# Linear attention with a bilinear feed-forward: the opening four units rescheduled (scaling on VectorE alone, idle matmuls in the kv bank, natural-k transposes together)

## The chip, the cores and the metric

One core of a Trainium2 chip runs the whole program. Times are device microseconds of an execution. A run is called slow when it is over 1.5% above the fastest of the same kernel. The kernel before needs 238.9 us (median of 3 runs, 238.88 to 238.95). Each profile is of one execution, and its clock starts at the first instruction of the span (237.3 us before).

## The reference, cut to what matters

```python
# B, H, S, D = 4, 8, 768, 64; decay lam per head
for b in range(nb):                                   # blocks of a sequence
    intra = einsum('bhic,bhjc->bhij', qb, kb) * Dmask     # lower triangle, lam**(i-j)
    intra = einsum('bhij,bhjd->bhid', intra, vb)
    inter = einsum('bhid,bhde->bhie', qb * lam_pow, kv_state)
    out[:, :, sl] = intra + inter
    kv_state = lam_block * kv_state + einsum('bhsd,bhse->bhde', kb * rev_pow, vb)
x = out.transpose(0, 2, 1, 3).reshape(B * S, H * D)       # 3072 x 512
y = ((x @ w_a) * (x @ w_b)) @ w_out                       # d_ff = 1536
```

The kernel works on 24 units of 128 rows (6 for each of 4 sequences). It scales q by lam to a power and k by lam to minus that power, so that the mask is a plain triangle. The feed-forward takes the units in groups of 4, 1, 2, 4, 4, 4, 4, 1; attention of later units is woven into the feed-forward of earlier ones. Only the first four units have nothing to hide behind. They are the **opening**, and the change is in it.

## The kernel before

PSUM, the memory that TensorE writes its results to, is handed out as seven banks in rotation (`ps_bank`) and an eighth for the kv states (`kv_bank`). A held bank is left out of the rotation. SBUF is the on-chip memory that holds the operands. An idle matmul (`warm`) is one whose result nobody reads.

```python
    def ps_bank(name, shape, dt, hold=False, ffn=False):
        i = bank["next"]
        while i in bank["held"] or (ffn and i == bank["ffn"]):
            i = (i + 1) % 7
        ...
    idle_ps = ps_bank("idle", [128, 512], F32, hold=True)   # target of idle matmuls: warm(n)
```

The opening itself: four packed inputs (q and k, half of the heads each) are scaled, by VectorE for three of four blocks and by GpSimd for the fourth, transposed on TensorE and copied to SBUF by ScalarE. Then come the scores, the natural-layout k, the states, and the outputs.

```python
        for eng, rs in ((nc.vector, slice(0, 3)), (nc.gpsimd, slice(3, 4))):      # in scale4
            ...eng.tensor_mul(...)
    ...
    for i in range(2):
        scale4("k", i); transpose4("k", i); warm(4)          # cut: one call per line; q likewise
    for u in range(n0):
        make_vb(u, "pool")
    scores4(0)                    # 16 matmuls into 4 banks, then 4 masks on VectorE
    natural_k(0, "act")           # 8 transposes into 1 bank, copied by ScalarE
    warm(4)
    scores4(1)
    natural_k(1, "act")
    sts = [ps_bank("kv0", ...), ps_bank("kv1", ...), kv_bank()]
    for hh in range(2):
        for u, ps in enumerate(sts):
            for w in range(u + 1):
                kv_mms(ps, w, range(2 * hh, 2 * hh + 2), w == 0)
            if hh:
                kv_copy(u, ps, ("act", "dve", "act")[u])
    for u in range(n0):
        inter(u); intra(u); warm(2)                          # cut: one call per line
        evac_o(u, *xTs[u], eng="dve" if u == 2 else "act")
    cast_w("a", 0, "both")        # half on VectorE, half on GpSimd
```

Outside the opening, until unit 6, the k of a unit is scaled on VectorE; q always, and k from unit 7 on, on GpSimd:

```python
    def prep_k(u):
        early = u < n0 + 3
        make_ks(u, "dve" if early else "pool")
        make_qs(u, "pool")
```

## Time and profile before

| what | value | read from |
|---|---|---|
| time, span | 238.9 us, 237.3 us | runs, page |
| TensorE busy | 227.0 us, 96% | page, part 1 |
| VectorE starts on the last k input | 10.35 us | timeline |
| first feed-forward matmul | 21.41 us | timeline |
| last ScalarE copy of the program | 233.99 to 234.26 us | timeline |

A line of the timeline reads: start, duration (of merged instructions, from first to last), engine and line of the code, operation, output<-input and form, and in brackets how long the engine had idled and what ended that. PE is TensorE's matmuls, PEld its weight loads, DVE is VectorE, ACT is ScalarE, POOL is GpSimd, and SPq the queue that issues the DMAs. The chain of waits goes back from the last instruction to what released it, step by step. The lines of before stand in the prediction below. Its state copies, which the change also moves, are these in the timeline:

```profile
17.57 0.74 ACT L371 CAST st<-kv 64x256 bf16<-64x256 f32 x2 [0.44 <-POOL wa_sb L159]
17.81 0.69 DVE L373 TENSOR_TENSOR st<-kv,bdiag 128x512 bf16<-128x512 f32 x1
```

kv1's copy on VectorE (second line) starts when the eighth mask ends.

### The profile page before, as it was taken

The page shows a single profiled execution, that of the slowest core. Times are in us where ns is not written, and L with a number is a line of the kernel's source. Part 1 is how long each engine was busy: PE and PEld are TensorE (multiplying, and loading weights), DVE is VectorE, ACT ScalarE, POOL GpSimd, SP SyncE. Part 2 cuts the span into 40 slices and gives each one's busy share as a digit, 9 for nine tenths or more (in the row PEclk, how much of TensorE's full clock was granted, in tenths as well). Part 3 has the DMA queues.
Part 4 walks back from the last instruction along what each step waited for, and adds up shares of the span by engine and source line. Part 5 has one row for each costly group of instructions (what it writes and reads, how often), then busy time and mean ns, then how long its engine had stood idle before and what let it go on. Part 6 is the DMA issues. An engine that isn't in the chain of part 4 may idle for free.

```text
span 237.3 us, 4532 instructions
## 1 busy us (share of the span) xinstructions
PE 227.0 (96%) x1758; PEld 126.8 (53%) x1781; DVE 113.5 (48%) x202; ACT 92.5 (39%) x171; POOL 53.6 (23%) x66
## 2 busy tenths in 40 slices
PE   7689999999999999999999999999999999999994
PEld 2365444447787754454554454544454544444493
DVE  0684656734647755775145575035565115332050
ACT  3556575037454542332133332143242242332161
POOL 6940001334334544203304503003300000000000
PEclk9999999999999999999999999999999999999999
DMA  4999999999969999995838939513220210000311
GB/s 156 298 291 349 350 369 281 285 217 297 212 157 209 220 185 241 251 196 105 187 125 197 199 64 241 133 57 89 44 47 0 88 69 24 0 0 3 128 48 47
DMA packets 94277, 38.31 MB, mean 161 GB/s; under 512 B 81200, under 2 KB 89776, under 8 KB 94256
## 3 DMA queue, kind: packets, MB, share of 16 engines
q1 hardware_dynamic: 94112, 38.02, 68.5%
q8 instruction: 14, 0.23, 0.4%
q14 instruction: 7, 0.06, 0.1%
q10 hardware_dynamic: 144, 0.00, 0.0%
HBM read 28.32 MB, written 6.29 MB: 146 GB/s over the span
## 4 chain that ended last, share of the span: by engine, by line
PE 88%; DMA 5%; ACT 2%; DVE 2%; issue 1%; SPq 1%; POOL 1%; DVEq 0%
PE a_ps L405 26%; PE b_ps L405 26%; PE op L426 26%; DMA k<-in_k_dram 3%; PE o_ps L337 3%; PE kq L308 2%; PE kvd L351 2%; PE o_ps L329 2%; DVE m L320 1%; DMA out_dram<-o_sb 1%; PE tps L294 1%; ACT o_sb L421 1%; SPq L206 1%; POOL scratch L495 1%; ACT xT L344 0%
## 5 line engine op out<-in xcount | busy, mean ns | idle before, releaser
L417 DVE TENSOR_TENSOR ab<-a_sb,b_ps 128x512 bf16<-128x512 bf16 (+2 forms) x96 | 52.4, 552 | 83.9 <-PE b_ps L405 62.3
L405 PE MATMUL a_ps<-xT,wa_sb 128*128 128x512 bf16 (+2 forms) x378 | 76.6, 325 | 1.4 <-ACT xT L344 0.6
L405 PE MATMUL b_ps<-xT,wb_sb 128*128 128x512 bf16 (+2 forms) x379 | 76.7, 325 | 0.2
L412 ACT CAST a_sb<-a_ps 128x512 bf16<-128x512 f32 (+2 forms) x96 | 45.5, 480 | 66.6 <-PE a_ps L405 64.7
L426 PE MATMUL op<-wo_sb,ab 128*128 128x512 bf16 (+2 forms) x300 | 64.3, 362 | 0.9 <-issue 0.5
L405 PEld LDWEIGHTS <-wb_sb 128*128 128x128 bf16 x384 | 34.5, 98 | 28.8 <-issue 0.2
L405 PEld LDWEIGHTS <-wa_sb 128*128 128x128 bf16 x384 | 33.6, 98 | 28.0 <-issue 1.1
L426 PEld LDWEIGHTS <-ab 128*128 128x128 bf16 x312 | 28.6, 98 | 30.2
L320 DVE TENSOR_TENSOR m<-kq,lotri 128x512 bf16<-128x512 f32 x48 | 29.8, 681 | 22.1 <-PE kq L308 20.4
L256 POOL TENSOR_TENSOR qk<-kf,lp_k 128x512 bf16<-128x512 f32 x17 | 17.9, 1051 | 80.2 <-issue 31.4
L421 ACT COPY o_sb<-op 128x512 f32<-128x512 f32 (+2 forms) x26 | 14.2, 553 | 37.2 <-PE op L426 36.7
L261 POOL TENSOR_TENSOR qk<-qf,lp_q 128x512 bf16<-128x512 f32 x20 | 22.0, 1099 | 23.8 <-DMA qf<-in_q_dram 23.8
L344 ACT CAST xT<-o_ps 128x512 bf16<-128x512 f32 x23 | 12.5, 589 | 17.0 <-PE o_ps L337 17.0
L373 DVE TENSOR_TENSOR st<-kvd,bdiag 128x512 bf16<-128x512 f32 x17 | 11.6, 682 | 3.8 <-PE kvd L351 3.8
L296 ACT COPY qkT<-tps 128x1024 bf16<-128x1024 bf16 x7 | 7.1, 1012 | 11.2 <-PE tps L294 11.2
L194 PE MATMUL idle<-idle_sb 128*128 128x128 bf16 (+1 forms) x41 | 8.2, 334 | 1.3 <-DVE idle_sb L189 1.3
L270 DVE CAST vb<-vf 128x512 bf16<-128x512 f32 x17 | 8.5, 499 | 0.0
L337 PE MATMUL o_ps<-m,vb 128*64 128x128 bf16 x192 | 8.2, 223 | 0.0
L329 PEld LDWEIGHTS <-st 128*128 128x128 bf16 x80 | 5.5, 98 | 2.6
L270 POOL CAST vb<-vf 128x512 bf16<-128x512 f32 x7 | 4.7, 673 | 8.7 <-DMA vf<-in_v_dram 8.7
L337 PEld LDWEIGHTS <-vb 128*64 128x64 bf16 x192 | 5.8, 109 | 1.6
L308 PE MATMUL kq<-qkT 64*128 64x128 bf16 x160 | 6.6, 218 | 0.0
(56 smaller groups left out, 88.9 us busy)
## 6 DMA issues: line engine op xcount, KB each, us to landing
vf<-in_v_dram SPq DMA_DIRECT2D x24, 256.0 KB, 5.0
out_dram<-o_sb SPq DMA_DIRECT2D x23, 256.0 KB, 2.2
qf<-in_q_dram SPq DMA_DIRECT2D x20, 256.0 KB, 4.4
kf<-in_k_dram SPq DMA_DIRECT2D x20, 256.0 KB, 4.6
wst<-in_moe_w_a_dram SPq DMA_DIRECT2D x6, 512.0 KB, 8.7
wst<-in_moe_w_b_dram SPq DMA_DIRECT2D x6, 512.0 KB, 8.7
wst<-in_moe_w_out_dram SPq DMA_DIRECT2D x6, 512.0 KB, 8.4
q<-in_q_dram SPq DMA_DIRECT2D x2, 512.0 KB, 5.5
```

The lines of the kernel that those rows point to most:

```text
L256: eng_of(eng).tensor_mul(qk[:, 1], raw.pop((u, "k")), lp_k[:, u % NB].to_broadcast([128, H, D]))
L261: eng_of(eng).tensor_mul(U[u]["qk"][:, 0], raw.pop((u, "q")), lp_q[:, u % NB].to_broadcast([128, H, D]))
L270: eng_of(eng).tensor_copy(vb, vf)
L320: nc.vector.tensor_mul(m, kq[i], lotri_bc)
L337: nc.tensor.matmul(d["o"][p, hp, :], lhsT=d["vb"][:, 2 * hp + i, :], rhs=d["m"](i, hp), start=(u % NB == 0 and hp == 0), stop=True, skip_g ...
L344: nc.scalar.copy(xT[:, :, col:col + BLK], o_ps)
L373: nc.vector.tensor_mul(st[:].rearrange("p hp i d -> p hp (i d)"), ps[:].rearrange("p hp i d -> p hp (i d)"), bdiag_bc)
L405: nc.tensor.matmul(ps[:, :gt], lhsT=w_sb[:, s, f * 128:(f + 1) * 128], rhs=xT[:, s, :gt], start=(s == 0), stop=(s == KS - 1))
L412: nc.scalar.copy(a_sb[:, :gt], ps[:, :gt])
L417: nc.vector.tensor_mul(ab[:, f, :gt], a_sb[:, :gt], ps[:, :gt])
L421: nc.scalar.copy(o_sb[:, lo:hi], op[:, lo:hi])
L426: nc.tensor.matmul(op[:, lo:hi], lhsT=ab[:, f, t * 128:(t + 1) * 128], rhs=wo_sb[:, f, lo:hi], start=(f == 0), stop=(f == FC - 1))
```

## The change

Intent: get the feed-forward started earlier. VectorE scales alone, in two parts per input, so that transposes of the first part can begin while the second is scaled. The idle matmuls write into the kv bank, which is unused until then, so that the rotation has seven banks. Both natural-k transposes go ahead of the second scores. kv1 is copied by ScalarE and kv2 by VectorE, twelve idle matmuls fall away, and GpSimd casts the whole first weight chunk.

```diff
-        elif eng == "both":
-            nc.vector.tensor_copy(dst[:, :, :128], t[:, :, :128])
+        elif eng == "pool":
+            nc.gpsimd.tensor_copy(dst[:, :, :128], t[:, :, :128])
...
-    idle_ps = ps_bank("idle", [128, 512], F32, hold=True)
+    idle_ps = kvps_pool.tile([128, 512], F32, name="idle", tag="kvd")
...
+    def load4(w, i):                       # in place of scale4 and transpose4
+        ...
+        for j in range(2):
+            hs = slice(4 * i + 2 * j, 4 * i + 2 * j + 2)
+            nc.vector.tensor_mul(...)      # 128 x 512
+            for r in range(PACK):
+                nc.tensor.transpose(tps[:, j, r, :], ..., ident)
...
+    for w in "qk":
+        for i in range(2):
+            load4(w, i)
+            warm(4)
...
     natural_k(0, "act")
-    warm(4)
+    natural_k(1, "act")
     scores4(1)
-    natural_k(1, "act")
...
-                kv_copy(u, ps, ("act", "dve", "act")[u])
+                kv_copy(u, ps, ("act", "act", "dve")[u])
...
-        warm(2)
...
-    cast_w("a", 0, "both")
+    cast_w("a", 0, "pool")
```

## The prediction

> **What bounds the kernel now.** I began with the page of the whole run. Its busy lines say that TensorE carries the kernel:
>
> ```profile
> PE 227.0 (96%) x1758; PEld 126.8 (53%) x1781; DVE 113.5 (48%) x202; ACT 92.5 (39%) x171; POOL 53.6 (23%) x66
> ...
> PEclk9999999999999999999999999999999999999999
> ```
>
> TensorE is busy for 96% of 237.3 us at full granted clock. From the first feed-forward matmul on it hardly waits: the view of TensorE's waits after 21 us lists 0.6 + 0.3 + 0.2 us. So the change, which touches only the first four units, can only move the moment at which that long stretch starts. Second view: the timeline of the opening, at the place where it starts.
>
> ```profile
> 20.60 0.42 DVE L158 CAST wa_sb<-wst 128x512 bf16<-128x512 f32 x1
> 20.78 0.58 ACT L344 CAST xT<-o_ps 128x512 bf16<-128x512 f32 x1 [0.59 <-PE o_ps L337]
> 21.41 1.89 PE L405 MATMUL a_ps<-xT,wa_sb 128*128 128x512 bf16 x7 [0.46 <-ACT xT L344]
> ```
>
> The feed-forward starts at 21.41 us, released by the last xT copy (ended 21.36); the VectorE half of the first weight cast ended at 21.02, just before. Third view: the chain of work that ended last, cut to the opening, names what leads to 21.41.
>
> ```profile
> 2.39 7.93 DMA k<-in_k_dram
> ...
> 10.40 1.39 POOL scratch L495
> ...
> 11.84 0.45 PE tk L505 x5
> 12.29 0.22 PE idle L194 x4
> 12.51 0.38 PE kq L533 x8
> ...
> 12.95 2.49 DVE m L320 x4
> 15.44 0.04 issue
> 15.48 0.62 PE tn L513 x8
> ...
> 16.12 1.02 ACT scratch L518
> ...
> 17.19 0.51 PE kv L351 x6
> ```
>
> The reader is to see three things: GpSimd's quarter of the scaling (1.39) is in the chain although VectorE does three quarters in 0.96; the second natural-k transpose (tn) waits for the fourth mask, because its PSUM bank is the one that mask reads; and its copy on ScalarE (1.02) then stands ahead of the second half of the kv matmuls. After that four units follow at 0.79 us each (17.96, 18.75, 19.54, 20.32), two idle matmuls in each.
>
> **What the Trainium skill says.** "SBUF — State Buffer", section Who interferes with whom: a VectorE instruction with two SBUF inputs contends with a GpSimd instruction that reads SBUF, and the loser waits for the whole instruction. The trace agrees: GpSimd scaled 256 elements in 1.38 us here, but 512 elements in 1.04 us elsewhere (L256); 1.38 is VectorE's 0.96 plus 0.42. "VectorE: DVE Perf Modes", section The TRN2 errata, gives an fp32 tensor_tensor (N+151)/0.96 ns: 957 for 768 and 691 for 512; the trace has 959 (L495) and 683 (L256 on VectorE). "TensorE: Matmul & The Clock Gate", section Step-by-step: matmuls stay in program order and only weight loads are pulled ahead; the trace agrees in that the kv matmuls, whose first inputs were there, came only after tn. The same page, HAM oscillation: the clock halves after a pause of about 3.4 us. No pause that long is in this trace after the start (clock 1.00 in all windows), so it shows neither side.
>
> **Part by part, as a new schedule of the opening.** I take durations, and the gaps after a release (0.05 to 0.06 us), from the rows above.
>
> Scaling. VectorE now does two parts of 512 elements. Eight masks of 512 took 4.87 us in a row, 0.61 apiece, 0.69 for a last one; so two parts take 0.61 + 0.69 = 1.30, and the first is ready after 0.69. The loads are not moved: VectorE waited for each of the four inputs (ready at 5.92, 7.29, 8.85, 10.35), and 10.15, the end of k0's second part, is before 10.35. k1's second part ends at 11.65; its four transposes start at 11.71. Before, the last five started at 11.83. The first transposes of scores now follow 0.55 later (was 0.61, one transpose of 0.056 less): 12.26 instead of 12.44. **Gain 0.18.** Copy of tk1: 12.15 to 13.16. Masks start at 12.77 and end at 12.77 + 7 x 0.61 + 0.69 = 17.7.
>
> Banks. With the idle matmuls in the kv bank, seven banks rotate instead of six. By the code: q in 0,1; k in 2,3; first scores 4,5,6,0; natural k in 1 and 2; second scores 3,4,5,6; kv0 in 0, kv1 in 1; outputs in 2,3,4,5. So natural k waits for no mask. Its two sets of transposes run at 12.81 and 13.26 (the second needs the tk1 copy, 13.16 + 0.06: in time). ScalarE copies them at 13.47 to 14.48 and 14.45 to 15.46; before, the second ended at 17.13. The second scores start at 13.71, wait for mask 3 (12.77 + 2 x 0.61 + 0.69 = 14.68) and end about 15.0.
>
> kv. kv0 sits in bank 0, which mask 4 frees at 12.77 + 3 x 0.61 + 0.69 = 15.29; so the wait for **mask 4 stays, now ahead of kv**. The 24 matmuls run from 15.36 without the pause in the middle: halves at 15.36 and 16.05 (each 12 x 0.056, about 0.70), end 16.75. Before, the second half started at 17.19. **Gain here 1.14** (the 0.18 is inside).
>
> States and outputs. Output 0 needs masks 5 and 6 (16.5): 16.75. kv0 on ScalarE starts 0.38 after the second half begins, as before (17.57 - 17.19): 16.43 to 17.17; kv1 is now on ScalarE too: to 17.91; kvd on VectorE behind the masks: 17.64 to 18.33. Without the two idle matmuls a unit needs about 0.66 instead of 0.79 (0.32 inter, from 18.43 to 18.75; 0.34 intra, from 18.75 to 19.09). Unit 1 starts at 17.23, unit 2 waits for kv1's copy, 17.97, and unit 3 follows at 18.63 (its state is there at 18.39); its intra part runs at 18.95, against 20.32 before. **Gain 1.37**; the ScalarE state copies cost two short waits in it, 0.13 us before unit 1 and 0.08 before unit 2.
>
> Start of the feed-forward. The last copy starts 0.46 after its intra part (before 20.78 - 20.32): 19.41, ends 20.00; first matmul 20.05. The first weight cast is two GpSimd pieces of 0.61 from its landing at 16.88: 18.10, so no longer near the gate. VectorE's second cast (wb) runs after output 2 (18.75 to 19.44) to 20.12; it is needed 1.73 later. 21.41 - 20.05 = **1.36 us**.
>
> After the start. The weights land at about 512 KB per 1.5 us (350 GB/s in the page's row) from 16.88, an estimate: the second a-chunk at 19.9, wanted at 23.7; each later one has more room, as TensorE uses one per 1.73. Then unit 4: its q landed at 40.74, v at 45.74, and its transposes ran at 48.83, so 1.36 earlier still leaves both in time. The last two output-weight casts, which ran at 45.0, may wait some tenths for their load, but their matmuls come at about 50.6. Bank numbers shift by three modulo seven, in the same order. So nothing gives the 1.36 back: 238.9 - 1.36 = 237.54, rounded to **237.5 us**.
>
> **Rivals.** (1) *The wait is replaced.* The masks stay on VectorE for 4.9 us and mask 4 still gates kv; ScalarE then holds four copies in a row for kv0 and kv1. If the kv copies or the mask-bound second scores take longer than in my schedule, the gain is 0.5 to 0.9: 238.0 to 238.4. For it: VectorE has no idle time between 12.95 and 18.5. Against: its end moves 0.2 only, but it stood at 17.8, 3.6 us ahead of the start of the feed-forward.
> (2) *Transfers hide it.* From 45 to 60 us the loads of units 5 to 7 are the slow side (GpSimd waits 1.8, 0.5, 1.5, 1.9 us for them). If the earlier feed-forward runs into them, the gain vanishes: 238.9. Against: TensorE needs unit 5 at 56.2 and unit 6 at 59.6, with k5 and k6 scaled on VectorE behind other VectorE work, without a load wait.
> (3) *The clock.* Fewer idle matmuls might let the granted clock fall. Twelve idle matmuls fall away (0.056 each, 0.7 us of activity in all); my schedule has no pause over 0.8 us between 12 and 20 us. If it happened, one halved window of 3.4 us would cost 1.7 us: 239.3. Chance 3%.
> (4) *More.* If the idle matmuls and gaps count for more than their issue time, the start could be at 19.6: 237.0.
>
> **Range and chances.** My schedule is the most likely; rival 1 at a third, giving 0.4 to 0.8 less, and rival 4 at a tenth. Range 236.9 to 238.4. For 2% the time must move by 4.8 us; the whole stretch from the last load to the feed-forward is 11 us, of which 4.9 are masks that stay. Faster by 2%: 0.01. Slower by 2%: 0.01. Within: 0.98.
>
> **What would show it.** Scaling rows on VectorE of 512 elements near 690 ns, none on GpSimd; the tk1 copy at 12.15; second natural-k copy ended by 15.5; kv matmuls in one row of 24 from about 15.4, released by a mask; kv1 on ScalarE ended near 17.9; first a_ps matmul at 20.05, released by ScalarE's xT copy. At 60 us and later everything should be earlier by the same 1.4. If the feed-forward starts earlier but the span does not follow, rival 2 is right; if the start moves by under 1.0, the schedule failed at the step whose time differs first; a PEclk digit under 9 would be rival 3.

## The result, and the profile after

The changed kernel took 237.97 us (median of 4 runs, 237.75 to 238.28) against 238.93 us in the same rounds; ratio 0.9959 with a 95% interval of 0.9942 to 0.9976. A ratio is the mean time of one kernel's fast runs over that of the other's of the same rounds, so not quite the ratio of the medians. It is clear of 1, below 2%, and within the range. A second measurement of the same kernel (below) gave 0.9944.

The chain of waits of the changed kernel in the opening, to be laid beside that of before:

```profile
2.39 7.90 DMA k<-in_k_dram
...
10.32 1.31 DVE scratch L495 x2
...
11.67 0.40 PE tk L500 x4
12.07 0.22 PE idle L194 x4
12.29 0.55 PE kq L530 x16
12.84 0.57 PE tn L510 x8
13.41 0.02 issue
13.43 1.94 ACT scratch L515 x2
15.37 0.48 PE kv L351 x6
```

GpSimd is gone from it, and the transposes tn no longer stand behind four masks. Both their copies (1.94 us) now run beside the second scores and the wait for the masks. The timeline at the end of the opening:

```profile
15.32 1.35 PEld L351 LDWEIGHTS <-scratch 128*128 128x128 bf16 x24 [0.45 <-issue]
...
16.39 1.51 ACT L371 CAST st<-kv 64x256 bf16<-64x256 f32 x4 [1.03 <-PE kv L351]
...
19.35 0.68 DVE L161 CAST wb_sb<-wst 128x1024 bf16<-128x1024 f32 x1
19.42 0.59 ACT L344 CAST xT<-o_ps 128x512 bf16<-128x512 f32 x1 [0.41 <-PE o_ps L337]
...
20.06 1.89 PE L405 MATMUL a_ps<-xT,wa_sb 128*128 128x512 bf16 x8 [0.68 <-DVE wb_sb L161]
```

All 24 kv weight loads are one row from 15.32. The first of them started before ScalarE's copies ended at 15.37, so it cannot have waited for them, though the chain says so. What it waited for is in the single records of the trace: mask 4 ended at 15.21, and TensorE's queue then had an instruction from 15.25 to 15.30 that waits on the semaphore of the masks. The feed-forward starts at 20.06 us, 1.35 us earlier. TensorE's busy share is again 96%:

```profile
PE 227.6 (96%) x1769; PEld 126.3 (53%) x1769; DVE 116.5 (49%) x205; ACT 92.4 (39%) x171; POOL 48.8 (21%) x63
```

| | before | changed | difference |
|---|---|---|---|
| first feed-forward matmul | 21.41 | 20.06 | -1.35 |
| end of the last ScalarE copy | 234.26 | 232.60 | -1.66 |
| span | 237.3 | 236.1 | -1.2 |
| tail (from that copy to the end of the span) | 3.06 | 3.53 | +0.47 |
| time, median | 238.93 | 237.97 | -0.96 |

So 1.35 us was gained at the start, another 0.3 came by near 75 us, and about 0.5 was lost after the last copy. Neither of the last two is in any step of the prediction, and that they partly cancel in this profile is luck. The queue of the stores shows it (before, then changed):

```profile
233.05 1.56 SPq L422 DMA_DIRECT2D out_dram<-o_sb  x3
```

```profile
231.40 2.05 SPq L422 DMA_DIRECT2D out_dram<-o_sb  x3
```

The same three stores took 1.56 us to issue before and 2.05 us now; the first landed 1.74 us after its issue before and 2.36 us now. Going through the DMA records of the trace one by one showed a second visitor: the queue named "instruction" in the page. Its packets of 16 KB on queue 8 start, in both traces, near the same counts of TensorE weight loads (the earlier ones up to 35 loads apart, the last one after 1752 and after 1753). The program before has 1781 loads, so the last of these fetches came 29 loads ahead of the end, at 231.76 us, and was over at 232.99, just ahead of the first store at 233.05. The changed program has 1769, so it came 16 loads ahead of the end, at 231.14, and lasted 1.45 us, to 232.60, while the first store was issued at 231.40. That is theory A of the experiments.

The granted clock of 0.998 is not an effect on the work. The windows of the changed kernel, by half microseconds (length, busy time and instruction count of each engine, then clock, DMA share and GB/s), show it falling after TensorE had finished at 232.3:

```profile
232.00:232.50 0.50, 0.30 (x6) 0.13 (x3) 0.00 (x0) 0.16 (x1) 0.00 (x0) 1.00 0.49 170
...
235.00:235.50 0.50, 0.00 (x0) 0.00 (x0) 0.00 (x0) 0.00 (x0) 0.00 (x0) 0.90 0.00 0
235.50:236.00 0.50, 0.00 (x0) 0.00 (x0) 0.00 (x0) 0.00 (x0) 0.00 (x0) 0.50 0.07 16
```

### The profile page after: what moved, and what is told of

Read it like the earlier page. It is cut to its first block, busy times and chain, and to the rows that moved or that the text cites. A ratio compares the mean times of both kernels' runs of the same rounds, so it can differ in the third digit from the quotient of the medians.

```text
span 236.1 us, 4532 instructions
## 1 busy us (share of the span) xinstructions
PE 227.6 (96%) x1769; PEld 126.3 (53%) x1769; DVE 116.5 (49%) x205; ACT 92.4 (39%) x171; POOL 48.8 (21%) x63
## 4 chain that ended last, share of the span: by engine, by line
PE 90%; DMA 3%; ACT 2%; DVE 2%; issue 1%; SPq 1%; DVEq 0%
PE a_ps L405 27%; PE b_ps L405 26%; PE op L426 26%; DMA k<-in_k_dram 3%; PE o_ps L337 3%; PE kq L308 2%; PE kvd L351 2%; PE o_ps L329 2%; PE tps L294 1%; ACT scratch L515 1%; ACT o_sb L421 1%; SPq L206 1%; DVE scratch L495 1%; PE kv L351 0%; DVE m L320 0%
## 5 line engine op out<-in xcount | busy, mean ns | idle before, releaser
L426 PE MATMUL op<-wo_sb,ab 128*128 128x512 bf16 (+2 forms) x312 | 65.6, 363 | 0.0
L261 POOL TENSOR_TENSOR qk<-qf,lp_q 128x512 bf16<-128x512 f32 x20 | 22.5, 1127 | 24.4 <-DMA qf<-in_q_dram 24.4
L373 DVE TENSOR_TENSOR st<-kvd,bdiag 128x512 bf16<-128x512 f32 x18 | 12.3, 683 | 3.8 <-PE kvd L351 3.8
L270 DVE CAST vb<-vf 128x512 bf16<-128x512 f32 x17 | 9.5, 561 | 0.0
L194 PE MATMUL idle<-idle_sb 128*128 128x128 bf16 (+1 forms) x29 | 7.2, 402 | 1.3 <-DVE idle_sb L189 1.3
```

What stands on the lines that cost most here:

```text
L261: eng_of(eng).tensor_mul(U[u]["qk"][:, 0], raw.pop((u, "q")), lp_q[:, u % NB].to_broadcast([128, H, D]))
L270: eng_of(eng).tensor_copy(vb, vf)
L373: nc.vector.tensor_mul(st[:].rearrange("p hp i d -> p hp (i d)"), ps[:].rearrange("p hp i d -> p hp (i d)"), bdiag_bc)
L426: nc.tensor.matmul(op[:, lo:hi], lhsT=ab[:, f, t * 128:(t + 1) * 128], rhs=wo_sb[:, f, lo:hi], start=(f == 0), stop=(f == FC - 1))
```

## The experiments

Twelve kernels ran (one of them the changed kernel again), on three chips; all were correct. For each, the start of the feed-forward is read from its profile. The load of the last k half lands up to 0.15 us apart from run to run, so I also give the **distance** from VectorE's start on that half to the first feed-forward matmul: 21.41 - 10.35 = 11.06 us before, 20.06 - 10.32 = 9.74 changed. "Tail" and "loads left" (after the last fetch began) are as above.

### Parts of the opening, put back one at a time

**Second natural-k transposes behind the second scores again (`order_back`).**

```diff
-    natural_k(1, "act")
     scores4(1)
+    natural_k(1, "act")
```

> The changed kernel with the second natural-k transposes again behind the second scores. With seven banks they fall on the bank that mask 3 frees (about 14.7 us), so ScalarE's second copy ends at about 16.4 instead of 15.4 and the second half of kv starts at 16.4 instead of 16.0: feed-forward at 20.4 to 20.5, +0.4 us (ratio to before about 0.9975). If the order is the heart of the change (it removes the whole 1.1 us wait) the start goes back to 21.0 or later. PE instruction count unchanged, so the tail should stay at 3.5 us.

Start 20.53 us, distance 10.10: +0.36, as expected. The timeline has the second half of kv waiting for the later copy:

```profile
16.48 0.51 PE L351 MATMUL kv<-vb,scratch 128*128 128x128 bf16 x6 [0.19 <-ACT scratch L515]
```

The order alone is worth a quarter of the gain, not the whole. The time, though, was 238.86 us (ratio 0.9997, 0.9983 to 1.0011), 0.5 us worse than the start explains; I come back to this at the port race. The tail, expected to stay at 3.5 us, was 3.10.

**A held bank for the idle matmuls again (`bank_back`).**

```diff
-    idle_ps = kvps_pool.tile([128, 512], F32, name="idle", tag="kvd")
+    idle_ps = ps_bank("idle", [128, 512], F32, hold=True)
```

> The changed kernel with the idle matmuls again in a held bank of their own, so six banks rotate. The natural-k transposes still find banks free (k's own); the second scores' last bank is freed by mask 4 (15.3) instead of mask 3 (14.7), they end at 15.6, and kv starts then instead of 15.36: feed-forward at about 20.3, +0.25 us (ratio about 0.997). If the seventh bank is what removes the wait, the start goes back to 21.0 or later.

Start 20.31, distance 9.97: +0.23. The second scores wait for a mask more, and kv starts at 15.59:

```profile
15.28 0.38 PE L530 MATMUL kq<-scratch 64*128 64x128 bf16 x7 [0.38 <-DVE m L320]
15.59 0.51 PE L351 MATMUL kv<-vb,scratch 128*128 128x128 bf16 x6
```

Ratio 0.997 (0.9956 to 0.9984), as expected.

**State copies on ScalarE, VectorE, ScalarE again (`kvcopy_back`).**

```diff
-                kv_copy(u, ps, ("act", "act", "dve")[u])
+                kv_copy(u, ps, ("act", "dve", "act")[u])
```

> The changed kernel with the state copies back on ScalarE, VectorE, ScalarE. kv1's copy then stands behind the eighth mask on VectorE (17.5 to 18.2) and unit 2 starts at about 18.26 instead of 17.96: feed-forward at 20.35, +0.3 us. If the copies do not matter, 20.05. Only the start is read sharply; the time may also move by the port race at 57 us.

Start 20.37, distance 10.04: +0.30. kv1's copy on VectorE waits for the last mask, and unit 2 for that copy:

```profile
17.53 0.68 DVE L373 TENSOR_TENSOR st<-kv,bdiag 128x512 bf16<-128x512 f32 x1
...
18.27 0.40 PE L329 MATMUL o_ps<-scratch,st 128*128 128x128 bf16 x4 [0.32 <-DVE st L373]
```

The time was 238.78 us (ratio 1.001, 0.9979 to 1.0041, with one run at 240.72 whose granted clock was 0.989): more lost than 0.3, as with `order_back`.

**Scaling shared with GpSimd again (`scale_back`).** The `scale4` and `transpose4` of before in place of `load4`.

> The changed kernel with VectorE's three quarters and GpSimd's quarter of the scaling as before. The last transposes of k start at 11.83 instead of 11.66 where the load lands as in the profile of before, and all that follows is 0.15 to 0.2 later: feed-forward at 20.2 to 20.3 (plus what a later k landing adds: read it as the distance from VectorE's start on the last k to the feed-forward, 9.73 us in the changed kernel, so 9.9 here). GpSimd's 256-element pieces take 1.38 again.

Start 20.23, distance 20.23 - 10.30 = 9.93: +0.19. The four GpSimd pieces again took 2.74 us a pair on q and 2.90 on k. Time 238.54 us, ratio 0.998 (0.9966 to 0.9993): again 0.3 to 0.4 us more than the start.

**First half of the weight cast on VectorE again (`cast_back`).**

```diff
         elif eng == "pool":
-            nc.gpsimd.tensor_copy(dst[:, :, :128], t[:, :, :128])
+            nc.vector.tensor_copy(dst[:, :, :128], t[:, :, :128])
```

> The changed kernel with the first half of the first weight cast again on VectorE, in its place behind the second unit-2 copy. The profile of the changed kernel names VectorE's cast of wb, which ended at 20.03, as what released the first feed-forward matmul at 20.06; ScalarE's last xT copy ended at 20.01. If the xT copy is the gate, the start stays at 20.05 although wb's cast now ends at about 20.4 (the half cast of 0.42 ends at about 19.8). If wb's cast is, the start moves to 20.45.

Start 20.04, distance 9.74: nothing lost. The timeline:

```profile
19.40 0.59 ACT L344 CAST xT<-o_ps 128x512 bf16<-128x512 f32 x1 [0.41 <-PE o_ps L337]
19.67 0.69 DVE L161 CAST wb_sb<-wst 128x1024 bf16<-128x1024 f32 x1
...
20.04 1.89 PE L405 MATMUL a_ps<-xT,wa_sb 128*128 128x512 bf16 x7 [0.68 <-ACT xT L344]
```

wb's cast now ends at 20.36, after the matmul has begun. So the profile's "<-DVE wb_sb" in the changed kernel named the event that came last, not the gate; the gate is ScalarE's last xT copy. This part of the change is worth nothing to the start. Ratio 0.9953 (0.9939 to 0.9966), the changed kernel's own.

**The twelve idle matmuls taken out of the kernel before, nothing else (`before_fewer_idle`).**

```diff
     natural_k(0, "act")
-    warm(4)
 ...
         intra(u)
-        warm(2)
```

> The kernel before without the four idle matmuls after the first natural-k transposes and the two after each of the four units (the same 12 that the change takes away), nothing else. The first four are hidden by the wait for mask 3; the pairs are in the chain of the units, so the feed-forward should start 0.3 to 0.4 us earlier (21.0 to 21.1). Theory A (instruction fetch): the program now has as many weight loads as the changed kernel (1769), so the fetch lies 16 loads before the end, the tail grows from 3.1 to 3.5 us and eats the gain: ratio 0.999 to 1.001. Theory B (tail by chance): tail about 3.1 and ratio 0.9985.

Start 21.12, distance 21.12 - 10.33 = 10.79: -0.27. Yet the time was 239.21 us, ratio 1.0008 (0.9995 to 1.0021): nothing gained. The tail was 3.40 us with 17 loads left, 0.34 us more than in the kernel before, as theory A says. It does not prove A by itself, because the start's gain was lost a first time near 58 us:

```profile
57.94 0.95 DVE L256 TENSOR_TENSOR qk<-kf,lp_k 128x512 bf16<-128x512 f32 x1
```

This instruction took 0.68 us in the kernel before, and TensorE waits 0.53 us for VectorE there instead of 0.27. It is the port race below, in a kernel whose start moved by only 0.27 us. (Near 75 us the profile is 0.13 us better than before, where the changed kernel's was 0.3 better.)

Together, the parts put back cost 0.19 (scaling) + 0.23 (bank) + 0.36 (order) + 0.30 (copies) + 0.00 (cast), and the idle matmuls 0.27 in the kernel before: 1.35 us, against 11.06 - 9.74 = 1.32 for the whole. The sum agrees almost too well, as parts in one chain can overlap.

### The tail

**Twelve idle matmuls more, in pauses (`pad`).**

```diff
-            warm(4)
+            warm(4 if (w, i) == ("k", 1) else 8)
```

> The changed kernel with four more idle matmuls after each of the first three scaled inputs: 12 matmuls and 12 weight loads more, in pauses of TensorE of 0.3 to 0.6 us that wait for VectorE, so the feed-forward should still start at 20.0 to 20.1 us. Theory A (the last 16 KB instruction fetch, which comes after some 1753 weight loads whatever the kernel, lies 16 loads before the end in the changed kernel and 29 before it in the kernel before, and now meets the output stores): the fetch moves back to 28 or 29 loads before the end, the tail after the last ScalarE copy goes from 3.5 back to 3.1 us, and the time falls by 0.4 to 0.5 us, to a ratio of 0.9935 to 0.9945. Theory B (the longer tail is chance of this one profile): tail anywhere, ratio unchanged at 0.996.

Distance 9.73, so they are hidden. The last fetch moved to 30 loads before the end, and the tail went back to 3.04 us; the three stores issue in 1.56 us again:

```profile
231.82 1.56 SPq L422 DMA_DIRECT2D out_dram<-o_sb  x3
```

The time did not fall clearly: 237.83 us, ratio 0.9951 (0.9938 to 0.9965), where theory A had 0.9945 at most. So the mechanism is as told, but 0.4 to 0.5 us was the worst of its cost and not its mean. All 14 profiles settle how it acts. "Overlap" is the end of the last fetch minus the issue of the first of the last three stores:

| kernel | loads left | overlap, us | tail, us |
|---|---|---|---|
| changed | 16 | 1.20 | 3.53 |
| scale_back | 15 | 1.10 | 3.42 |
| before_fewer_idle | 17 | 1.09 | 3.40 |
| cast_back | 16 | 1.07 | 3.38 |
| bank_back | 14 | 0.98 | 3.29 |
| order_back | 15 | 0.77 | 3.10 |
| kvcopy_back | 15 | 0.73 | 3.04 |
| after_again | 18 | 0.71 | 3.03 |
| k6_pool | 16 | 0.68 | 3.04 |
| before, pad, k6_pool_pad, before_k6_pool, faster | 29 to 31 | below 0 | 3.02 to 3.06 |

Above an overlap of about 0.73 us the tail grows one for one; below, nothing happens. How long the fetch takes (0.93 to 1.45 us in these nine) and at which load it begins (14 to 18 left) decide, and both differ from run to run: the changed kernel's two profiles have 1.45 us with 16 left and 1.06 us with 18 left. The mean tail of the nine is 3.25 us, from which I estimate that the shorter program costs 0.2 us on average. Theory B (chance) is thus wrong as to the cause and right as to the single profile.

**The changed kernel once more (`after_again`).**

> The changed kernel as it is, to see what repeats: feed-forward at 20.0 to 20.2 us, ratio 0.995 to 0.9965. The last instruction fetch again 16 loads before the end; the tail 3.05 us if the fetch took under 1.0 us, 3.3 to 3.5 if longer (it was so in the runs so far). VectorE's scaling of unit 6 takes either 0.68 or about 1.4 us, and TensorE's wait for ab at 57.8 is 0.3 or about 1.0 accordingly.

Start 20.06, distance 9.73, as expected. Three expectations missed: the tail was 3.03 with a fetch of 1.06 us, where I had drawn the line at 1.0; VectorE's unit 6 took 0.75 us, neither 0.68 nor 1.4; and the kernel was a little faster than I allowed, 237.75 us (6 runs, 237.24 to 238.41), ratio 0.9944 (0.993 to 0.9959), the medians 1.28 us apart.

### The port race at 57 us

Why did three put-back kernels lose more time than their start? In each, TensorE has 1.0 to 1.1 us of waiting for VectorE's ab near 58 us, where the changed kernel has 0.3. The timelines there, first the changed kernel's GpSimd and VectorE, then those of `order_back`:

```profile
56.94 1.52 POOL L261 TENSOR_TENSOR qk<-qf,lp_q 128x512 bf16<-128x512 f32 x1
```

```profile
56.87 0.68 DVE L256 TENSOR_TENSOR qk<-kf,lp_k 128x512 bf16<-128x512 f32 x1
```

```profile
57.19 1.04 POOL L261 TENSOR_TENSOR qk<-qf,lp_q 128x512 bf16<-128x512 f32 x1
```

```profile
57.34 1.43 DVE L256 TENSOR_TENSOR qk<-kf,lp_k 128x512 bf16<-128x512 f32 x1
58.70 0.67 DVE L417 TENSOR_TENSOR ab<-a_sb,b_ps 128x128 bf16<-128x128 bf16 x3
```

VectorE scales k of unit 6, GpSimd q of unit 7, each with two SBUF inputs: the contention that the prediction quotes from the Trainium skill. Who starts first runs at full speed or nearly (0.68 to 0.76, or 1.04; it was 0.75 or 0.76 where GpSimd's scaling of unit 7's k still had 0.2 us to run), the other takes 1.4 to 1.6 us. In the changed kernel VectorE won by 0.07 us. In `order_back` GpSimd won by 0.15, in `kvcopy_back` by 0.07 (VectorE 1.53 us), in `scale_back` by 0.11 (1.48 us), and in `before_fewer_idle` by 0.64 (0.95 us, as only 0.41 us of GpSimd's was left). In each of these four VectorE was done 0.54 to 0.56 us after GpSimd. In the kernel before VectorE was at 58.23, after GpSimd's end at 57.88, so there was no race. GpSimd's start is set by the landing of unit 7's k (55.8 to 56.2 us in all), which the change does not move, and VectorE's by the feed-forward, which it does. Beyond the opening this is what an earlier start runs into.

**Unit 6's k on GpSimd (`k6_pool`).**

```diff
-        early = u < n0 + 3
+        early = u < n0 + 2
```

> The changed kernel with the k scaling of unit 6 on GpSimd instead of VectorE. In the profile of the run with the order put back this VectorE instruction took 1.43 us instead of 0.68, because GpSimd's scaling of unit 7, which starts when its load lands (about 56 us), had begun 0.15 us earlier; TensorE then waited 1.02 us for VectorE's ab. Theory P (the earlier feed-forward brings unit 6's scaling on VectorE, at 58.2 in the kernel before and 56.9 now, into the time of GpSimd's unit 7, and who comes first is settled by tenths of a us): without it TensorE's wait at 57.8 (0.28 us in the changed kernel's profile) shrinks to under 0.1, and the runs lie closer together; time 0.3 to 0.6 us below the changed kernel's, ratio to before 0.9935 to 0.995. Rival (the spread and the missing part come from the tail and the loads alone): the wait stays or moves to another instruction, ratio 0.996.

Start 20.08; the wait for ab is gone from the list of waits, TensorE is 0.3 us ahead of the changed kernel at 57.5 us. 237.28 us, ratio 0.9934 (0.9921 to 0.9948). The runs did not lie closer together (236.84 to 237.88), so the race is not what spreads them.

**The same in the kernel before (`before_k6_pool`).**

> The kernel before with unit 6's k scaling on GpSimd, nothing else. In the profile of before this instruction ran at 58.23 us, after GpSimd's unit 7 (to 57.9), in 0.68 us, so there is no collision to take away; only TensorE's wait of 0.27 us for ab at 59.2 goes: ratio 0.9985 to 0.999. If the gain of moving it were independent of the change (the same 0.3 us and spread), the ratio would be 0.9975 or less.

I missed here: 238.6 us, ratio 0.9976 (0.9963 to 0.9988), where I had allowed 0.9985 at best for my theory. TensorE was 0.34 us nearer to the changed kernel after 58 us, and another 0.2 near 75 us. So moving this scaling pays without any race, and `k6_pool`'s gain may be mostly that. That the part near 75 us comes of the scaling is not shown: `after_again`, with the scaling on VectorE, has it too. The race is shown in three put-back kernels and in `before_fewer_idle`; how often it costs the changed kernel its 0.75 us stays open, since both its profiles won it, by 0.07 and 0.16 us.

**Both remedies (`k6_pool_pad`).**

> Unit 6's k scaling on GpSimd and the 12 hidden idle matmuls together, on top of the changed kernel. If both losses are as told, nothing of the gain at the start is lost: tail 3.05 us with the fetch 28 to 30 loads before the end, no wait for ab at 57.8; ratio about 0.0015 below that of the run with unit 6 on GpSimd alone, 0.992 to 0.9935, and the runs close together. If the tail is by chance, it is no faster than that run (0.9934).

237.41 us, ratio 0.9926 (0.9913 to 0.9939); tail 3.04 with 31 loads left, no wait for ab. The step from 0.9934 has the right sign and size, but the intervals overlap, so by time alone it is not shown.

### A version that beats both

**What the opening still waits for, taken away (`faster`).**

```diff
-            warm(4)
+            warm(0 if (w, i) == ("k", 1) else 10)
 ...
-    sts = [ps_bank("kv0", ...), ps_bank("kv1", ...), kv_bank()]
+    kv1, kv0 = (ps_bank(n, [128, HP, 2, D], F32) for n in ("kv1", "kv0"))
+    sts = [kv0, kv1, kv_bank()]
     for hh in range(2):
-        for u, ps in enumerate(sts):
+        for u in ((2, 0, 1), (0, 1, 2))[hh]:
+            ps = sts[u]
 ...
+        # unit 3: its xT copy in two halves (heads 0-3, 4-7) on ScalarE
 ...
-        early = u < n0 + 3
+        early = u < n0 + 2
```

> On top of the changed kernel: unit 6's k scaling on GpSimd; no idle matmuls after the last k transposes and ten after each of the other three scaled inputs (0.22 us off the chain, 14 weight loads more); the first half of kv begins with the state of unit 2, whose bank is free, and mask 4's bank is needed 0.45 us later (0.3 us); the last xT copy in two halves on ScalarE, so the first two feed-forward matmuls need only the first half (0.2 us). Feed-forward at 19.3 to 19.5 us instead of 20.05, tail 3.05: time 236.3 to 236.8, ratio 0.989 to 0.991. If the masks bound the rest, 19.6 and 0.9915.

236.83 us (236.53 to 237.9), ratio 0.9906 (0.9892 to 0.9921), against 0.9944 for the changed kernel in the same rounds. The four edits were not run apart. The feed-forward started at 19.29 us, with the first half of the copy as its gate, and the tail was 3.04 us:

```profile
18.86 0.65 ACT L567 CAST xT<-o_ps 128x256 bf16<-128x256 f32 x2 [0.41 <-PE o_ps L337]
...
19.29 0.59 PE L405 MATMUL a_ps<-xT,wa_sb 128*128 128x512 bf16 x2 [0.47 <-ACT xT L567]
```

Its profile caught the slowest of its five runs, and shows the next bound, in the chain of waits:

```profile
96.80 5.51 DMA qkT<-qk
102.31 0.05 issue
102.36 0.40 PE kq L308 x8
```

From unit 11 on q and k are transposed by DMA. In this run TensorE waited for unit 14's transpose, issued at 96.80 and landed at 102.31: 1.6 us, more than the whole of what `faster` had gained on the changed kernel by then. In the other profiles the same transpose landed between 100.0 and 102.7 us; the kernel before wanted it at 103.3, the changed one at 101.6. So the room for a landing at 102.7 is there before and not after the change.

## Why the prediction was right

- *Start of the feed-forward*, predicted 20.05 us: 20.06 in both profiles. That it is this close is in part luck, as the last k half came 0.02 to 0.03 us earlier than in the kernel before; the distance is the fairer measure, 9.70 in the schedule, 9.74 and 9.73 measured. The steps below it held as well: tk copy at 12.15 (12.10), masks from 12.77 (12.72), second natural-k copy ended by 15.46 (15.36), kv from 15.36 (15.36), first state copy at 16.43 (16.39), last unit's intra part at 18.95 (18.96). The put-back kernels confirm each part: the scaling at 0.19 (0.18 in the schedule), order, bank and copies at 0.36, 0.23 and 0.30.
- *Slips that cost nothing.* Its masks are too long: 7 x 0.61 + 0.69 is 4.96, not the 4.87 measured (the later ones follow 0.60 apart), so mask 4 ended at 15.21 and not 15.29. The view with waits of 0.6 + 0.3 + 0.2 us ended at 60 us; to the end of the program TensorE's waits are 0.6 + 0.5 + 0.3. And 237.54 + 1.7 in rival 3 is 239.2.
- *Rival 1*, the wait replaced: mask 4 does stand ahead of kv, as the schedule itself had it, but it took no more than foreseen. The time of 237.97 us is close to what rival 1 would have given (238.0 to 238.4), so the time alone could not tell the two apart; the start at 20.06 does.
- *"So nothing gives the 1.36 back"* is the step that was only nearly right. Measured were 0.96 us in one set of rounds and 1.28 in the other. Three things can take some of it: the fetch meeting the stores (0 to 0.5 us, 0.2 in the mean, shown), the port race (0.75 to 0.85 us when lost, shown in neighbours of the changed kernel), and the DMA transposes at 102 us (shown only in `faster`). Near 75 us TensorE pauses none to four times for some 0.16 us, three times in the profile of before, once and not at all in the two of the changed kernel, four times in `k6_pool_pad`. The pauses are 0.60 us apart, as masks are, so TensorE probably waits for banks that masks free; this was not taken apart.
- *Rival 2*, transfers: I looked for it at units 5 to 7 and against TensorE. It exists in two other forms, a load that times GpSimd against VectorE, and transposes at unit 14.
- *Rival 3*, the clock: wrong; it fell only 3.1 us after the last matmul. By the clock records of the other profiles it fell 2.1 us (`k6_pool`) to 5.1 us (`before_k6_pool`) after it, so this does not bear out one length of pause, such as the 3.4 us that the prediction quotes. *Rival 4*, more than the schedule at the start: wrong.
- What stays open: the share of each of the three in the changed kernel's spread, 237.24 to 238.41 over its ten runs, against 238.80 to 239.42 for the kernel before in all rounds.

## What to carry to other kernels

A schedule worked out from measured durations, with every bank and its last reader written down, can hit the start of the next stage to 0.04 us; check each "released by" in such a schedule for events that merely came last. Work that is moved earlier meets whatever is timed by loads, so list those first: shared ports, transfers with little slack. And the number of instructions alone can move an instruction fetch into the last stores, so compare the tail of the program before crediting a small change in time to the change.

## What the Trainium skill lacked or had wrong

- "DMA: Bandwidth & Descriptors", section Issuing engines are not separate DMA queues, says that DMAs started by the scalar, sync or gpsimd engine run on the same 16 DMA engines and interleave. It does not list instruction fetches among them. "Runtime: NRT & Kernel Launch", section Instruction fetch mechanics, has the fetches (blocks of 16 KiB through a DMA queue of the sequencer's own) and calls their cost mostly hidden. Neither says that one can meet the last stores: here a 16 KB fetch of 0.93 to 1.45 us near the end of TensorE's program went with a tail of 3.03 to 3.53 us, against 3.02 to 3.06 where it was over before the stores.
- "SBUF — State Buffer", section Who interferes with whom, was right, and the port race rests on it: VectorE's 0.68 us became 1.43 to 1.53 and GpSimd's 1.04 became 1.49 to 1.57, whichever started second.
- "TensorE: Matmul & The Clock Gate", section Back-to-back issue gap, gives about 81 ns per matmul for 128 columns and 131 ns for 512 in a stream of weight loads and matmuls. Here such pairs went at 0.45 us for 8 transposes (56 ns) and 0.86 us for 4 matmuls of 512 (216 ns), in the chain of waits of before.
